# Issuing the v loads of 18 chunks from ScalarE's queue, in a gated-attention and gMLP kernel

## The chip, the cores and the metric

The kernel runs on one core of a Trainium2 chip. A core has five engines, each with a queue of its own that it works off strictly in order: TensorE (PE), VectorE (DVE), ScalarE (ACT), GpSimd (POOL) and SyncE (SP). SP computes nothing; it issues DMAs. The metric is the device time of one execution in microseconds (us), as the median of several runs.

## The reference

The inputs q, k, v and alpha have the shape (4, 8, 768, 48): batch, heads, steps, head size, in float32. For each batch and head a gated linear attention runs over the steps:

```
state = alpha[t][:, None] * state + outer(k[t], v[t])
y[t]  = q[t] @ state
```

The heads are then put side by side to x (4 x 768 x 384), and a gated MLP follows:

```
h = relu(x @ w_in);  u, v = h[..., :512], h[..., 512:]
v_n = (v - mean(v)) / sqrt(var(v) + 1e-6)
v_s = w_spatial @ v_n + b_spatial        # over the 768 steps
out = (u * v_s) @ w_out
```

## The kernel before, in words

**Tiles and stages.** The 768 steps of a batch are cut into chunks of 128, so there are 24 chunks, numbered 0 to 23 over the four batches. Chunks 0 to 5 are handled two at a time (`pair`, line 388), chunks 6 to 23 singly (`first`, line 590). A chunk has four loads: alpha (tile `ac`), k (`kc`), q (`qc`) and v (`vc`). A single chunk's load is 192 KB in pieces of 192 bytes (line 602); a pair's is 384 KB in pieces of 384 bytes (line 406). The tiles of a load rotate through three buffers, each of which holds two chunks, so a load waits until the reader of the chunks six places earlier is done.

For a single chunk the steps are these. ACT takes the logarithm of alpha (`ln`, line 616) and PE makes its running sum (`cum`, 622 and 625). ACT takes exponentials of it (`einv` 634, `ebc` 641, `eexp` 651). POOL multiplies k by one of them (`kt`, 646) and DVE multiplies q by the other (`qt`, 656). v is cast to bf16 (`vb`, 663, by ACT or POOL, through the helper at line 196 or 198). PE transposes kt and qt (`trk`, 672 and 674), and the result is copied to SBUF (`ev`). PE makes the scores (`sc`, 704), DVE masks them (`m`, 715), PE updates the state from kt and vb (`upd`, 690) and makes y (`y`, 726 and 732). DVE and POOL keep the state (`z`, `S`, `sb`; lines 325 to 340). y is copied, transposed and copied to `xT` (`xs`, `xt`, `xe`; lines 353 to 372).

The MLP of a batch runs in groups of matmuls at line 778: `v` and `u` (x by the two halves of w_in; the eviction with relu is on ACT or DVE), the normalisation of v (`bn`, `rs`, `vn`), `s` (the spatial product with w_spatial, evicted by DVE at 920, and a product with u on POOL or DVE at 933), and `o` (the product with w_out, evicted by ACT). Then the 128 x 384 result is stored (line 980). The weights come in six pieces of 768 KB (line 1008): two of w_in, three of w_spatial, one of w_out. They go through two buffers, are cast to bf16, and w_spatial is transposed on PE.

**What sets the order.** Every step is an operation with a number and the engines that may do it. The constant `PLAN` (line 57) is an order table written out in full: a word such as `P54:512` says that operation 54 comes next and is done by PE (P PE, D DVE, A ACT, G POOL, S an issue on SP, Q the landing of a DMA, which emits nothing), and that before it 512 columns of junk matmul are run on PE (line 188). `replay` (line 111) emits the operations in this order. Each engine's queue therefore has its operations in the order of the table, and an engine that waits for one operation holds up all that follow it in its queue. A DMA is two operations, its issue and its landing (`dma`, line 295); the issue is on SP unless said otherwise.

**Queues.** All loads and stores but one are issued by SP; POOL issues the load of b_spatial (line 1028).

Of the kernel before, what the change touches and what calls it, by code (L numbers as in the profile page):

```python
# [57 lines left out]
S34 S96 G0 S36 S38 Q35 D1 Q97 S100 A42 Q37 S98 P43:512:512:512:512:512:512:512:512:512:352 A104 G32 P54:512 Q33 A44  # L58
Q39 S40 P116 A55 D47 A56 P105:128 A57 G58 A45 A46 D2 Q101 S166 P50:512:96 A107 A106 P61:256 A117 D51 A118 A108 D59
A119 Q99 S102 D48 P63:512:512:512:512 A64 D121 P243:512:224 P52 D110 P125 Q41 S4 D53 D62 A126 P73:512:512:160 G120  # L60
P114 A244 D74 P76 Q167 G109 S168 P123:160 D115 D75 A49 G60 P112:512:512:192 D77 Q103 A113 P65:224 S170 D78 A124
P135:512 D66 A174 P79:96 D136 G67 Q5 S172 P138 A80 D137 G68 P69:224 A111 D70 G122 D139 P83:512:352 G71 D140 P175 G72
Q169 S9 P127 A177 A84 P81 D128 P141 A82 G129 A176 P85 Q171 S303 P186 A142 D7 G6 A86 P131 D8 A178 P143 D130 G179 A187
P87 Q173 S14 A188 D132 P90 A88 G133 D180 P145 A91 G189 D190 Q10 S305 A144 P182 D92 P184 A146 G134 P194 A185 P149
D195 G181 A183 D89 P147 P192 G191 A148 P200 G3 Q304 A193 S307 P245:128 D201 P160 A150 D202 Q15 P203 P196 D12 A13 D11
A246 D205 P156:512:512:512:512:320 S18 A93 P154 D197 A311 Q306 S309 D204 A161 G198 P152 A157 P312 D16 Q308 G199 S335
A155 P206 D151 A313 G17 Q19 A153 P210 D94 A314 A207 G315 D162 S22 P158 A316 P208 A211 P233 D317 A209 P231 D95 A163
P212 Q310 P319 D232 S337 A213 P214 D164 A234 G20 D320 Q336 P223 S370 A215 G21 D159 P217 Q23 D216 S339 P227 A218 P235
A224 P237 D219 A228 P225 A318 P229 D165 A343 Q338 D236 S341 P325 A220 D238 P321 A226 P344 Q371 D222 P259 A230 S372
D221 P251 A346 A345 D326 Q340 A24 G25 P255 S374 D322 P256 D327 A348 Q342 P260 G347 S412 D257 P239 A378 Q373 P328  # L70
G323 P241 S410 A240 D349 P379 P252 Q375 D261 A380 S414 P247 A381 D242 A329 G262 Q413 P248 A350 D253 S376 A383 P351
D249 G324 Q411 P353 P330 D352 S26 P267 A331 G258 P268 D384 Q415 S445 P357 G382 D269 P275 Q377 A418 D354 S416 P276
D359 G355 P386 Q27 D358 G356 S447 P271 D387 P419 G254 P272 A421 D277 A420 P392 A423 G422 P332 D424 P360 D273 G250
Q446 A333 S449 P426 D393 A361 P263 G274 A385 Q417 D394 P264 S477 A427 P388 P362 D265 Q448 P395 S479 A363 D31 P432
G266 D30 A396 P364 Q450 D29 A28 S481 D389 A453 D334 P397 P279 G390 Q478 A398 S572 G391 A365 P454 D433 P399 Q480 A455
D434 G278 S451 A456 A458 P408 A400 Q482 P283 D459 G425 S574 A280 D401 G457 P404 A284 Q573 P287 S604 A485 D409 G270
A405 Q452 P428 D366 P486 A288 S576 P435 A487 P461 Q575 A436 G488 S483 P291 A367 D462 A489 Q605 P295 D369 S578 A292
D429 P437 D490 A296 Q577 P467 G430 S606 A438 P406 D368 G431 A580 D469 P492 Q484 A407 S608 P581 D468 G460 P439 A582
Q579 D493 A583 S641 A585 P463 G584 P470 D464 A612 Q607 P494 D586 A471 S639 P402 G465 D495 A440 P472 Q609 G466 P613
A403 D496 S679 P588 A615 A614 G491 P299 D441 Q642 A473 S610 G587 A617 P497 G616 D589 Q640 P474 A498 S681 D618 A442  # L80
P590 P499 Q680 D591 P594 A500 S715 P620 G592 D596 A300 Q611 P501 A475 D443 S645 A476 D621 P514 Q682 P508 S643 D595
A502 P512 A503 Q716 G619 D444 S683 D515 P626 A647 P597 D504 P524 Q646 A513 S717 P528 A598 A509 Q644 D627 P540 S685
A505 P648 A687 P599 D507 Q684 P510 A600 D506 S719 P688 A649 D628 P525 Q718 A650 A690 A652 G651 S747 P541 D526 A723
P622 Q686 P529 D542 A689 G593 S749 A692 P544 D623 D530 Q720 A654 G691 P545 S751 D693 P629 D653 Q748 G624 P724 S841
P695 D511 A725 G543 P655 A630 Q750 D546 P516 S873 A726 A728 G527 P631 D696 A656 Q752 P517 S721 G625 P657 D729 P601
A632 Q842 D658 A694 G531 S843 D518 P661 A602 P701 Q874 D662 P633 G727 A755 S845 D663 P520 Q722 A634 G519 D702 S875
P756 P521 A757 Q844 D703 G659 P664 S877 P536 D522 G758 A665 Q846 P731 D635 A759 S753 P532 G660 A849 Q876 D760 P666
P697 S912 G547 P533 A667 D698 A732 Q878 P537 D534 S908 G523 P704 D538 P850 Q754 A705 P668 D603 G699 S948 A851 P762
A852 Q913 A854 G853 S847 P677 A669 D855 P706 Q909 A730 P548 G700 D678 S301 A707 D763 P733 Q949 P857 A549 D734 S879
A881 P708 D858 G735 A670 Q848 P737 S983 G535 P764 A709 D739 P863 Q302 P671 A710 S914 G736 D738 Q880 P552 S910 A636  # L90
D765 G761 P740 A672 Q984 G539 D766 P882 S950 A741 P556 A553 D864 Q915 G856 P767 S1015 A557 D865 P742 P560 A884 A768
Q911 D711 A883 S952 P673 A886 G885 P564 Q951 A743 D887 S985 A916 P769 D637 G888 P859 A561 Q1016 P675 D674 G923 S954
A770 P744 D676 A712 Q953 P777 D860 S987 A745 D638 P889 G861 Q986 A565 P771 S1019 A956 D890 A778 P779 Q955 D746 A772
S289 P917 P891 P957 A919 Q988 A918 D713 P866 S989 D714 A959 P781 A780 G920 D773 A921 Q1020 P793 S1021 A867 P797 D892
A1023 Q290 D922 P568 A774 S293 Q990 A958 P924 S1017 D776 A961 P785 D775 G960 Q1022 A782 D925 P868 S285 P786 A869
D962 G893 P794 Q294 A963 D787 G862 P798 A569 Q1018 D795 A991 P870 S570 G788 D799 S297 Q286 P926 A871 P895 D927 G796
P930 Q571 D897 P801 Q298 G894 P802 D896 P783 D932 G928 P992 D931 P789 A994 A993 P898 D803 A784 G995 P1024 A996 P966
P933 A899 D967 P790 D997 A934 G968 P809 A1025 D791 G998 A1027 P900 P810 D872 G1026 A901 P964 D1028 P999 G800 A965
P813 D1000 G792 P935 P1030 D811 A936 P814 D1031 G804 P1001 P817 D1002 G929 D815 P970 A818 P1005 D971 P1032 G1003
P942 G1029 D972 P821 G816 D1006 P805 A822 D1007 G969 P973 P937 D1033 A974 G1004 P806 D1034 A938 P975 P1008 D807 A976  # L100
P902 D943 A1009 G808 D939 P1035 A903 P1010 P977 G812 A1036 D904 P944 A978 P940 A1011 D979 P1037 P829 A1038 D945 A905
P825 D907 P1012 A826 A980 P1039 A941 D981 P1049 A1013 D982 P946 D906 A1040 D1014 P1045 A830 P1051 A947 S831 D1041
A1046 P1047 S281 P1053 S823 D1050 A1042 Q832 S558 P1057 A1052 D1044 Q282 S827 P1077 A1048 D1043 Q824 S562 P1065 Q559
P1078 S819 P1066 Q828 P1061 Q563 D1067 P1054 Q820 G1068 P1058 D1055 P1062 D1059 G1056 P1069 D1060 P1070 D1063 P1073
D1079 P833 P1074 A834 P1081 D1075 S835 P1082 D1064 S550 G1076 P837 S554 D1071 Q836 S566 P1084 D1080 A838 Q551 G1072
P1088 S839 Q555 D1083 A1085 P1092 Q567 S1086 A1089 Q840 P1100 S1090 A1093 Q1087 P1096 S1094 A1101 Q1091 P1104 S1102
A1097 Q1095 S1098 A1105 Q1103 S1106 Q1099 Q1107
# [16 lines left out]
def kernel(  # L124
# [12 lines left out]
    nc = tc.nc  # L137

    B, H, S, D = q.shape
    C = 128  # L140
# [50 lines left out]

    ENG = {"ACT": nc.scalar, "DVE": nc.vector, "POOL": nc.gpsimd}
# [195 lines left out]
    def pair(j):  # L388
# [13 lines left out]
        def load(name, src):  # L402
            def emit(_):
                t = st[name] = io_pool.tile([128, 2, H, D], FP32, name=name).rearrange(
                    "p a h d -> p (a h d)").rearrange("p (h a d) -> p h a d", h=H, a=2)
                nc.sync.dma_start(
                    out=t.rearrange("p h a d -> p h (a d)"),
                    in_=src[b, :, t0:t0 + 2 * C, :].rearrange("h (p a) d -> p h (a d)", a=2))
            return emit
# [180 lines left out]
    def first(i):  # L590
# [6 lines left out]
        def load(name, src):  # L597
            def emit(_):
                if i % 2 == 0:
                    T[i + 1][name + "2"] = st[name + "2"] = io_pool.tile([128, 2, H, D], FP32, name=name)  # L600
                t = st[name] = st[name + "2"][:, i % 2]
                nc.sync.dma_start(out=t, in_=src[b, :, t0:t0 + C, :].rearrange("h s d -> s h d"))  # L602
            return emit
# [6 lines left out]
        dma(("vc", i), LD, load("vc", v), io_users("vb", j), P + 0.3)  # L610
# [340 lines left out]
    def second_o(b, tt):  # L951
# [27 lines left out]
        def store(_):  # L979
            nc.sync.dma_start(out=out[b, tt * 128:(tt + 1) * 128, :], in_=hold["o"])  # L980
# [19 lines left out]
    def fetch(key, prio, to, src):  # L1000
# [4 lines left out]
        def load(_):  # L1005
            flat = raws.tile([128, n * cols], FP32, name="raw_w")
            hold["w"] = flat.rearrange("p (n f) -> p n f", n=n)
            nc.sync.dma_start(out=hold["w"], in_=src)
# [75 lines left out]
```

## Time and profile before

| | |
|---|---|
| median of 3 runs | 147.5 us (146.93 to 147.93) |
| the profiled execution | 148.49 us, its span 146.7 us |
| granted TensorE clock, mean | 0.997 of full |
| PE busy | 138.6 us (94%) |
| DVE, ACT, POOL busy | 120.6, 107.8, 87.1 us |
| matmuls of the groups (line 778) | 38% of the chain that ended last |
| junk matmuls (line 188) | 66, 11.8 us busy |
| issues of vc on SP, single chunks | 18, median 4.2 us from issue to landing |
| HBM read, written | 23.60 MB, 4.72 MB |

The profile page is made from one execution. Its span runs from the first to the last instruction of the program; the rest of the execution's time lies around it. The page gives the busy time of each engine, the same in 40 slices, the DMA queues, the chain of work that ended last (followed back from the last instruction, at each step to what released it), and the costliest groups of instructions. A group is named by line, engine, operation and out<-in; after the bar stand its busy time, the mean of one in ns, and the idle time of the engine just before them with what ended it. An issue of a DMA is shown on the queue of its issuer ("SPq") and is not counted as busy. PE's busy time is modelled, so a PE that is 99% busy is not at its peak; how much useful work is done is counted in columns of the matmuls instead.

### The profile page before, as it was taken

The numbers are of one execution on the slowest core, as the hardware profiler recorded it, in microseconds if no ns is written. First come the engines' busy times: TensorE is split into PE (matmuls) and PEld (weight loads), VectorE is DVE, ScalarE is ACT, GpSimd is POOL, SyncE is SP. The second block draws the span as 40 slices with busy tenths as digits, with TensorE's granted clock in tenths as the row PEclk, the third lists the DMA queues.
The fourth block names the chain that finished last, engine by engine and source line by source line (L and its number), as shares of the span: only waits on it lengthen the run. The fifth ranks groups of instructions, "written<-read, shape, count | busy, mean of one in ns | idle before, by whom it ended". The sixth has DMA issues, their size and how long they took to land.

```text
span 146.7 us, 4486 instructions
## 1 busy us (share of the span) xinstructions
PE 138.6 (94%) x1702; PEld 92.3 (63%) x1715; DVE 120.6 (82%) x260; ACT 107.8 (73%) x271; POOL 87.1 (59%) x148
## 2 busy tenths in 40 slices
PE   6999999999999999995998999999999999999990
PEld 3567776676666666773666577666667766566550
DVE  6578989979999899994977898988989999767820
ACT  3595779988984599995996889999948548860160
POOL 5726487574258959773139987853597994004320
PEclk9999999999999999999999999999999999999998
DMA  4999998978997999997998999999998000063384
GB/s 109 268 261 263 330 259 245 332 183 210 312 216 151 267 208 199 197 197 141 191 213 163 221 194 206 186 210 188 202 222 258 22 0 0 4 242 138 135 293 161
DMA packets 93014, 28.61 MB, mean 195 GB/s; under 512 B 87872, under 2 KB 91456, under 8 KB 92992
## 3 DMA queue, kind: packets, MB, share of 16 engines
q1 hardware_dynamic: 92960, 28.32, 83.4%
q8 instruction: 13, 0.21, 0.6%
q14 instruction: 9, 0.07, 0.2%
q0 software_dynamic: 32, 0.00, 0.0%
HBM read 23.60 MB, written 4.72 MB: 193 GB/s over the span
## 4 chain that ended last, share of the span: by engine, by line
PE 64%; DMA 12%; DVE 8%; ACT 5%; POOL 4%; issue 3%; SPq 1%; DVEq 0%; ACTq 0%; POOLq 0%
PE bank L778 38%; DMA qc<-in_q_dram 7%; PE bank L188 6%; DMA raw_w<-in_moe_w_spatial_dram 5%; PE bank L704 2%; POOL gT L933 2%; PE bank L672 2%; PE bank L732 2%; PE bank L361 2%; PE bank L674 2%; PE bank L690 1%; DVE qt L656 1%; PE bank L492 1%; PE bank L428 1%; SPq L602 1%
## 5 line engine op out<-in xcount | busy, mean ns | idle before, releaser
L778 PE MATMUL bank<-w_spT,vn 128*128 128x384 bf16 x192 | 36.3, 326 | 0.0
L933 POOL TENSOR_TENSOR gT<-vsb,uT 128x384 bf16<-128x384 f32 x28 | 25.8, 932 | 16.1 <-DVE vsb L920 15.5
L778 PEld LDWEIGHTS <-vn 128*128 128x128 bf16 x192 | 17.3, 97 | 10.0 <-issue 0.2
L715 DVE TENSOR_TENSOR ptm<-bank,mask 128x512 bf16<-128x512 f32 x36 | 22.8, 681 | 0.5 <-PE bank L704 0.5
L646 POOL TENSOR_TENSOR kt<-kc,binv 128x384 bf16<-128x384 f32 x18 | 16.7, 928 | 7.4 <-ACT bc L641 4.4
L920 DVE TENSOR_TENSOR vsb<-bank,bsp_bc 128x384 f32<-128x384 f32 x31 | 16.7, 552 | 3.8 <-PE bank L778 2.8
L778 PE MATMUL bank<-xT,w_in 128*128 128x384 bf16 x96 | 19.2, 327 | 0.0
L778 PE MATMUL bank<-w_out_sb,gT 128*128 128x384 bf16 x96 | 18.4, 326 | 0.1
L778 PE MATMUL bank<-w_in,xT 128*128 128x512 bf16 x59 | 17.1, 379 | 1.0 <-issue 0.5
L332 POOL TENSOR_TENSOR state<-state,bc 128x192 f32<-128x192 f32 x20 | 10.2, 511 | 8.2 <-DVE state L327 4.9
L198 POOL CAST sbd<-state 64x192 bf16<-64x192 f32 x38 | 12.9, 340 | 2.0
L196 ACT COPY xT<-bank 128x384 bf16<-128x384 bf16 x24 | 11.7, 487 | 3.0 <-PE bank L361 2.4
L839 DVE BATCH_NORM_STATS2 stats<-v_sb 128x6 f32<-128x512 bf16 x20 | 13.6, 682 | 0.3 <-ACT v_sb L202 0.3
L202 ACT ACTIVATE v_sb<-bank 128x512 bf16<-128x512 f32 x20 | 11.7, 598 | 2.6 <-PE bank L778 2.2
L656 DVE TENSOR_TENSOR qt<-qc,bank 128x384 bf16<-128x384 f32 x18 | 9.8, 548 | 4.4 <-DMA qc<-in_q_dram 2.9
L188 PE MATMUL bank<-junk 128*128 128x384 bf16 (+5 forms) x66 | 11.8, 313 | 1.3 <-DVE junk L231 1.3
L198 DVE COPY kqT<-bank 128x1024 bf16<-128x1024 bf16 (+1 forms) x19 | 11.6, 614 | 1.5 <-PE bank L674 0.5
L196 ACT COPY o_sb<-bank 128x384 f32<-128x384 f32 x9 | 4.3, 480 | 11.4 <-PE bank L778 11.4
L778 PEld LDWEIGHTS <-w_in 128*128 128x128 bf16 x96 | 8.7, 98 | 6.1
L778 PEld LDWEIGHTS <-gT 128*128 128x128 bf16 x96 | 9.0, 97 | 5.4 <-issue 0.3
L196 ACT CAST x_sb<-bank 128x384 bf16<-128x384 f32 x24 | 11.6, 488 | 1.0 <-PE bank L732 0.5
L871 DVE TENSOR_SCALAR vn<-v_sb,mvs,rstd 128x512 bf16<-128x512 bf16 x24 | 10.6, 467 | 2.0 <-ACT rstd L864 1.9
(124 smaller groups left out, 299.1 us busy)
## 6 DMA issues: line engine op xcount, KB each, us to landing
ac<-in_alpha_dram SPq DMA_DIRECT2D x18, 192.0 KB, 4.1
kc<-in_k_dram SPq DMA_DIRECT2D x18, 192.0 KB, 3.9
qc<-in_q_dram SPq DMA_DIRECT2D x18, 192.0 KB, 3.8
vc<-in_v_dram SPq DMA_DIRECT2D x18, 192.0 KB, 4.2
raw_w<-in_moe_w_spatial_dram SPq DMA_DIRECT2D x3, 768.0 KB, 7.6
out_dram<-raw_w SPq DMA_DIRECT2D x12, 192.0 KB, 2.3
out_dram<-o_sb SPq DMA_DIRECT2D x9, 192.0 KB, 2.4
raw_w<-in_moe_w_in_dram SPq DMA_DIRECT2D x2, 768.0 KB, 7.6
```

Of the source, the lines that this page charges most:

```text
L188: nc.tensor.matmul(out=flat[:, 0:n], lhsT=junk[:, 0:128], rhs=junk[:, 0:n], start=True, stop=True)
L196: nc.scalar.copy(out=out, in_=in_)
L198: ENG[eng].tensor_copy(out=out, in_=in_)
L202: nc.scalar.activation(out=out, in_=in_, func=AF.Relu)
L646: ENG[eng].tensor_mul(out=k_blocks(kt3)[:, :, :, 0:D], in0=quad(st["kc"]), in1=st["binv"])
L656: nc.vector.tensor_mul(out=qt[:, :, ::-1, 0:D], in0=quad(st["qc"]), in1=st["cv"])
L715: nc.vector.tensor_tensor(out=st["ptm"][:, s], in0=st[f"pt{s}"], in1=mask4, op=ALU.mult)
L778: return lambda ps: nc.tensor.matmul(out=out(ps), lhsT=lhsT(), rhs=rhs(), start=start, stop=stop)
L839: nc.vector.bn_stats(out=stats, in_=d["v_sb"][:, tt, :])
L871: nc.vector.tensor_scalar(out=d["vn"][:, t, :], in0=d["v_sb"][:, t, :], scalar1=d["mvs"][:, t, 0:1], scalar2=d["rstd"][:, t:t + 1], op0=AL ...
L920: nc.vector.tensor_tensor(out=hold["vs"], in0=ps[:, 0:TH], in1=bsp_bc[:, th, :], op=ALU.add)
L933: ENG[eng].tensor_tensor(out=bt[b]["gT"][:, dsl, cols], in0=hold["vs"], in1=bt[b]["uT"][:, dsl, cols], op=ALU.mult)
```

## The change

The loads of v of the single chunks (6 to 23) are issued by ACT's queue instead of SP's: `dma(("vc", i), ...)` gets `eng="ACT"`, and the function that issues takes the queue from the engine that the table names. The 18 issues become instructions of ACT, in ACT's order. The loads of the pairs (also v), of the weights, and the stores stay on SP.

The table is replaced by another one for two queues. It has the same 1108 operations. Beside the 18 issues it moves these:

- casts of v: ACT 7 to 4, POOL 11 to 14 (single chunks); ACT 2 to 3, POOL 4 to 3 (pairs)
- `ev` of single chunks: ACT 4 to 6, DVE 14 to 12; of the pairs' k: ACT 4 to 2, DVE 2 to 4; of their q: ACT 3 to 4, DVE 3 to 2
- k product of the pairs: POOL 5 to 2, DVE 1 to 4
- casts of weights: w_in ACT 1 to 3, DVE 4 to 2; w_spatial ACT 1 to 0, DVE 1 to 2; w_out DVE 3 to 2, POOL 0 to 1
- transposed w_spatial: ACT 2 to 3, DVE 4 to 3; one state copy and one product with u from POOL to DVE
- junk columns: 16224 to 18976

The order of issues changes as well. SP's queue begins like this before and after (the number is the chunk, the first of two for a pair; `w_sp` is w_spatial):

```
before: ac0 ac2 kc0 qc0 qc2 kc2 vc0 ac4 vc2 w_in.1 kc4 qc4 vc4 w_in.0 ac6 w_sp.0 kc6 qc6 w_sp.1 vc6 ac7 w_sp.2 kc7 ac8 qc7 vc7 kc8 qc8
after:  vc0 ac0 ac2 kc0 kc2 qc0 qc2 vc2 ac4 qc4 w_in.1 kc4 ac6 vc4 ac7 w_in.0 ac8 w_sp.0 qc6 kc6 ac9 qc7 kc7 w_sp.1 w_sp.2 kc8 qc8
```

In the new table the issues of vc6, vc7 and vc8 on ACT stand ahead of w_in.0, of kc6 and of kc6, in that order. Around them ACT's queue reads: `xs.0 vc.6.issue eexpp.2.1 ... xe.3 xe.2 vc.7.issue vc.8.issue vbp.2.1 ln.6`.

The diff, with the table cut to its first line:

```
 PLAN = """
-S34 S96 G0 S36 S38 Q35 D1 Q97 S100 A42 Q37 S98 P43:512:512:512:512:512:512:512:512:512:352 A104 G32 P54:512 Q33 A44
...
+S40 S34 G0 S96 S36 Q41 D1 Q35 S98 D2 Q97 S38 A42 G32 A49 G60 Q37 S100
...
+    QUEUE = {"SP": nc.sync, "ACT": nc.scalar}
     ENG = {"ACT": nc.scalar, "DVE": nc.vector, "POOL": nc.gpsimd}
...
         def load(name, src):
-            def emit(_):
+            def emit(eng):
                 if i % 2 == 0:
                     T[i + 1][name + "2"] = st[name + "2"] = io_pool.tile([128, 2, H, D], FP32, name=name)
                 t = st[name] = st[name + "2"][:, i % 2]
-                nc.sync.dma_start(out=t, in_=src[b, :, t0:t0 + C, :].rearrange("h s d -> s h d"))
+                QUEUE[eng].dma_start(out=t, in_=src[b, :, t0:t0 + C, :].rearrange("h s d -> s h d"))
...
-        dma(("vc", i), LD, load("vc", v), io_users("vb", j), P + 0.3)
+        dma(("vc", i), LD, load("vc", v), io_users("vb", j), P + 0.3, eng="ACT")
```

The loads of the pairs, the stores and the weights' loads get the same `QUEUE[eng]`, with SP as the engine.

## The prediction

> **What bounds the kernel now.** I read the page first: span, engine rows, DMA row.
>
> ```profile
> span 146.7 us, 4486 instructions
> ...
> PE 138.6 (94%) x1702; PEld 92.3 (63%) x1715; DVE 120.6 (82%) x260; ACT 107.8 (73%) x271; POOL 87.1 (59%) x148
> ...
> DMA  4999998978997999997998999999998000063384
> ...
> GB/s 109 268 261 263 330 259 245 332 183 210 312 216 151 267 208 199 197 197 141 191 213 163 221 194 206 186 210 188 202 222 258 22 0 0 4 242 138 135 293 161
> ...
> q1 hardware_dynamic: 92960, 28.32, 83.4%
> ```
>
> The DMA engines are full from the start to about 113 us and then nearly idle. Before that the rate sits near 200 GB/s wherever only chunk loads run. The profiled execution took 148.49 us, its span 146.7, the runs' median is 147.5: I work with differences against the span and add them to the median.
>
> Next, the busy time by stage (columns: PE, PEld, DVE, ACT, POOL, clock, DMA share, GB/s):
>
> ```profile
> 24.00:56.00 32.00, 31.35 (x407) 21.30 (x409) 29.92 (x64) 25.98 (x64) 20.65 (x34) 1.00 0.98 236
> 56.00:80.00 24.00, 21.95 (x275) 14.90 (x276) 19.47 (x45) 20.77 (x59) 14.63 (x26) 1.00 0.96 187
> 80.00:112.00 32.00, 31.78 (x402) 21.83 (x406) 28.63 (x62) 27.77 (x74) 23.40 (x38) 1.00 0.98 201
> 112.00:146.70 34.70, 30.91 (x267) 19.20 (x265) 23.70 (x50) 17.18 (x41) 14.29 (x22) 0.99 0.34 123
> ```
>
> TensorE (PE) loses 2.05 us between 56 and 80 us (24.00 - 21.95), 0.65 between 24 and 56, and almost nothing from 80 on. ACT is idle for 6.02 + 3.23 + 4.23 = 13.5 us between 24 and 112. Who makes PE wait is in the chain in order of time, and in the view of the v tiles:
>
> ```profile
> 63.81 5.16 DMA qc<-in_q_dram
> 68.97 0.03 issue
> 69.00 0.02 DVEq L656
> 69.02 0.04 issue
> 69.06 0.55 DVE qt L656
> ...
> 73.89 4.87 DMA qc<-in_q_dram
> ...
> 78.86 1.03 DVE qt L656 x2
> ...
> 125.97 17.06 PE bank L778 x101
> ```
>
> ```profile
> L602 SPq DMA_DIRECT2D vc<-in_v_dram x18: 425/888/2058, 30.2 to 106.6; - x18
> ...
>   PE bank L690: 1.1, 1
> ...
> DMA to landing us min/median/max: 3.8/4.3/7.5
> ```
>
> So the kernel is PE-bound, with PE work held up wherever a load is late. 101 matmuls in 17.06 us are 0.17 us each. With 384 columns in 0.163 us (three in 0.49 in the chain), the order tables of before and after hold the same useful PE work, 125.8 us by their columns: the new time is decided only by how much PE waits and by the start and the end.
>
> **The change part by part.**
>
> *The transfers themselves: 0 us.* The bytes and the 192-byte pieces stay. Two windows of 8 us give the price of a load: one single chunk's load, 196,608 B, takes 0.99 us at 199 GB/s (56 to 64 us), a pair's takes 1.48 us at 266 GB/s (8 to 16 us). The engines' share there is 1.01 and more, so a second queue finds no free engine: a v load that goes sooner makes a k or q load later by 0.99 us. What it can fill is the rest, a DMA share of 0.96 to 0.98 in the three stages: 0.02 x 32 + 0.04 x 24 + 0.02 x 32 = 2.2 us at most. [...]
>
> *The order of loads on SP: +1.8 us.* The new table is another order, not the old one minus 18 issues. By the table's places, chunk 6 (the first single chunk) suffers. Ahead of its k load now stand six more single loads: alpha of 7 and 8, q of 6, and v of 6, 7 and 8 on ACT's queue. That is 6 x 0.99 = 5.9 us.
>
> ```profile
> 23.06 0.59 SPq L602 DMA_DIRECT2D kc<-in_k_dram  x1
> ...
> DMA to landing us min/median/max: 3.9/4.8/7.8
> ...
> ```
>
> ```profile
> 31.62 0.90 POOL L646 TENSOR_TENSOR kt<-kc,binv 128x384 bf16<-128x384 f32 x1
> ```
>
> ```profile
> 33.60 0.39 PE L672 MATMUL bank<-ident,kt 128*128 128x128 bf16 x4
> ```
>
> Before, this k load was issued at 23.06 and took 7.8 us (the longest of four in the k tiles' view), so it landed at 30.9; its product on POOL started at 31.6 and its transposes on PE at 33.6. After, the landing is 30.9 + 5.9 = 36.8, or 3 x 0.99 less (33.8) if ACT reaches its v issues later than the table thinks. With 0.90 of POOL and 0.2 of hand-over the transposes start at 37.9, or at 34.9. The PE work ahead of them in the table is 21.1 us against 20.5 before, so by there PE has waited 37.9 - 33.6 - 0.6 = 3.7 us more, or 34.9 - 33.6 - 0.6 = 0.7: 2.2 in the middle. The weights move too: w_spatial's second part has 8 more single loads ahead of it (7.9 us), w_out about as many; the matmuls that need them stand 2 to 4.5 us later in PE's table and 2.2 us later in time, which covers all but a few tenths. From chunk 7 on the sets loaded are about the same. The old stall (2.05 us at 56 to 80) was for v of chunk 12 and q of 13 and 15. In the new table q of 15 comes some 6.5 us later by its place, but PE has 5.2 us more work ahead of chunk 15's transposes (68.0 against 62.8) and is 2.2 us later: nearly even. I book a gain of 0.4 there: 2.2 - 0.4 = +1.8. Ends: -2.7 (all of 2.05 + 0.65 goes, chunk 6 covered) and +3.7.
>
> *The start: 0 us.* SP's first load is now v of the first pair, so the first alpha lands one pair load (1.48 us) later and q of the first pair two later (3.0). The late chunk 6 covers it, as do 2752 more junk columns. Without that cover the start costs up to 1.5 us, and what replaces it as late is w_in's first half, also behind three more single loads.
>
> *ACT: +1.7 us.* ACT gets 18 issues. No row shows an issue on ACT. Lower end: the shortest of the 72 issues on SP at this line, 0.376 us (least of the queue ahead of it): 6.8 us. Upper end: 1.44 us, the median for v of a pair in the same view, which has to wait for transfers ahead: 26 us. ACT's own queue holds few transfers, but the 16 engines are those that SP keeps full, so I take the median of the same instruction, 0.89: 16.0 us. Beside this, moved evictions add 1.7 us to ACT by its mean durations (3 v casts fewer at 0.41, 2 kqT copies more at 0.94, 2 weight casts more at 0.50, and small ones). Up to the ln of chunk 12 ACT has no trouble: 46.2 us of work and 6 issues, against 46.8 us that before were done at 62.1 us. From there to the xT copy of chunk 18 (before: 44.3 us, of them 39.2 busy) it has 42.8 us and 11 issues: 52.6 us at 0.89, 8.3 over; at 0.376 it is 46.9, 2.6 over. What queues behind each issue is ln, exp and the evictions; for these wait kt on POOL, qt on DVE and then PE. Not all of it is on the path: 2 us are given by the later loads, o and u evictions (12 x 0.4 us in that stretch) have no near reader, and PE has S and O groups to run meanwhile. Between 0 (2.6 - 2) and 6.3 (8.3 - 2) I take 1.7, nearer to the low end, as 4.8 us are such evictions. [...]
>
> *POOL and DVE: 0 us.* POOL gets 3 more v casts (0.50 each) and 3 kt of pairs fewer (0.91); DVE gets these 3. POOL is busy 59%; on DVE it falls in the start, where PE runs junk; if not covered, +0.6 each.
>
> *SP: 0 us.* It issues 18 fewer, but its issues are as long as the DMA lets them be (mean 0.99 us, as the transfer), so they only spread.
>
> Sum: 147.5 + 0 + 1.8 + 0 + 1.7 = **151.0 us**.
>
> **The rivals.**
>
> *The v wait goes and nothing replaces it (faster).* A v load no longer stands behind SP's full queue (median 4.3 us to landing); the 1.1 us that PE waited for a v cast and the q waits vanish because q moves up. 147.5 - 2.7 = 144.8. Against it: the DMA share of 0.96 to 1.01. It decides if chunk 6's transposes start by 34.5 and PE loses under 0.7 us between 56 and 80.
>
> *ACT becomes the bound (slower still).* With issues of 1.2 us, 42.8 + 13.2 = 56.0 against 44.3: 11.7 over, less 2 from the loads and 4.8 of evictions that may wait, 4.9 us, on top of 1.8: 154.2; at 1.44 it is 156.8. For it: SP's issues last up to 3 us when transfers stand ahead of them. Against it: ACT's queue is its own. It decides from about 0.9 us an issue.
>
> *Nothing moves (about 147.5).* Chunk 6's delay is eaten by two queues filling the 2.2 us of gaps, and issues are short. The split of issues itself is certain from the program's order, so "the change does not take place" is excluded.
>
> **How the numbers follow.** About 1% (1.5 us, three runs of before spread over 1.0) is what a measurement can tell. Forecast (149.0 to 153.5): 0.47. ACT as bound (over 153.5): 0.18. Faster (under 146.0): 0.18. Nothing moves (146.0 to 149.0): 0.17. So faster 0.18, same 0.17, slower 0.65. The range 145.0 to 157.0 takes in all but the ends of the outer two (0.07 below, 0.06 above); the likeliest case alone is 149.0 to 153.5.
>
> **What would show it.** Right: single loads still about 0.99 us apart at 195 to 205 GB/s; transposes of chunk 6 at 35 to 38 us; useful PE work equal, PE's loss moved from 56-80 us to 24-40 us; ACT issues of 0.4 to 1.2 us and ACT idle under 5 us from 62 to 112. Wrong: a DMA rate over 210 GB/s in the chunk stage (two queues do move more), ACT issues near 0.1 us, or a last k or q load that lands clearly before 111 us.

## The result and the profile after

The kernel after takes 152.94 us (median of 4 runs, 151.44 to 153.35), the kernel before in the same session 147.72 us (146.93 to 148.13). The ratio is 1.034, with a 95% interval of 1.026 to 1.043: the change makes the kernel about 5 us slower. Ratios and their intervals come from all executions but those over 1.5% above the fastest of their kernel, so they can differ a little from the quotient of the medians. The profiled execution of after took 153.35 us, its span 151.6 us against 146.7.

The page of after, with the rows that the prediction showed of before:

```profile
span 151.6 us, 4500 instructions
...
PE 140.8 (93%) x1712; PEld 92.5 (61%) x1725; DVE 122.6 (81%) x262; ACT 109.3 (72%) x272; POOL 83.7 (55%) x145
...
DMA  4999999998989999799999999970590200049134
GB/s 118 265 261 263 275 271 280 349 243 150 335 210 202 218 292 219 148 216 219 192 262 199 229 229 226 229 133 0 160 205 9 52 0 2 4 147 366 60 144 167
...
q1 hardware_dynamic: 74240, 24.78, 68.7%
q10 hardware_dynamic: 18720, 3.54, 12.0%
```

Read the last two rows first: there are two queues now, and q10 carries the 18 loads of v (3.54 MB). The DMA row drops at about 101 us, and the rate to 0: SP then stands at a store whose data isn't there yet, with a single load (q of chunk 23) behind it. The last load of k lands at 100.8 us, before at 113.0. By 101 us all but 6 of the 72 single loads have landed, before all but 11; q of chunk 23 and v of chunks 20 to 23 are issued only from 106 us on, and the last of them lands at 118.9 us. Most loads are done sooner, and yet the span is 4.9 us longer. So the loads' throughput isn't what became worse.

The busy time by stage (PE, PEld, DVE, ACT, POOL, clock, DMA share, GB/s):

```profile
0.00:24.00 24.00, 22.09 (x348) 14.77 (x348) 17.83 (x42) 15.47 (x35) 12.83 (x33) 1.00 1.10 244
24.00:56.00 32.00, 29.73 (x405) 20.37 (x407) 27.71 (x61) 25.51 (x62) 17.80 (x28) 1.00 1.04 250
56.00:80.00 24.00, 21.54 (x265) 13.74 (x263) 19.24 (x41) 19.90 (x53) 15.61 (x29) 1.00 1.05 214
80.00:112.00 32.00, 31.84 (x375) 21.39 (x378) 27.37 (x61) 28.77 (x81) 21.05 (x34) 1.00 0.85 179
112.00:151.60 39.60, 35.58 (x334) 22.18 (x335) 30.46 (x62) 19.62 (x46) 16.36 (x25) 1.00 0.30 98
```

PE loses 2.27 us between 24 and 56 (before: 0.65) and 2.46 between 56 and 80 (before: 2.05). The rate is higher than before in both stages: 250 against 236 and 214 against 187 GB/s.

Who makes PE wait in the first of them is in the chain in order of time (start, length, what):

```profile
26.89 9.38 DMA kc<-in_k_dram
...
36.41 0.92 POOL kt L648
...
37.38 0.40 PE bank L674 x4
```

This is chunk 6: its k load lands at 36.28 us, its product on POOL follows, and its transposes start at 37.4 us, against 33.6 before. But PE itself stood still for it for less than that. PE's timeline gives the idle time in front of these transposes in brackets:

```profile
37.38 0.40 PE L674 MATMUL bank<-ident,kt 128*128 128x128 bf16 x4 [0.93 <-POOL kt L648]
```

Up to 0.93 us before, PE was working off what stands ahead of them in its order. So the late load holds PE up by 0.93 us at most; the rest of the 3.8 us PE brings with it.

In the second stage, the chain has a row that before couldn't have: an issue on ACT that waits for a load. The waits of ACT give the size (us in total, times, longest):

```profile
63.03 5.08 DMA kc<-in_k_dram
68.11 0.02 issue
68.13 0.37 ACTq L604
```

```profile
ACT raw_w L198 <- DMA kc<-in_k_dram: 2.4, 1, 2.4
```

ACT stands still for 2.4 us in front of an eviction (`raw_w`). PE soon waits for what ACT does next, the copy to `x_sb`:

```profile
69.51 0.34 PE L363 MATMUL bank<-ident,x_sb 128*128 128x128 bf16 x3 [1.72 <-ACT x_sb L198]
```

The eviction needs no k load. What waited was the issue ahead of it in ACT's queue, the v load of chunk 13; it starts 0.02 us after a load of k has landed. That v issue needs no k load either. The trace's records of the issues, with the semaphores that they raise and wait for, show why it waits. In before, the 114 DMAs that SP issues raise eight completion semaphores (counters that tell of a landing) in strict turn, and each issue from the ninth on waits, by itself or in a semaphore instruction ahead of it, for its own semaphore: for the DMA eight issues earlier. That DMA was issued 9.1 us earlier in the median and had landed at least 2.8 us before, so no issue stood still for it. In after, the 96 DMAs of SP and the 18 of ACT raise eight semaphores between them, 14 or 15 DMAs each, and each issue again waits for its own. The v issue of chunk 13 raises number 103, and the DMA before it on 103 is SP's load of k of chunk 13, issued only 5.1 us earlier, at 63.03, and landed at 68.11 us. It works the other way too: SP's issue of k of chunk 7, also on 103, starts 0.02 us after the landing of v of chunk 7, which ACT had issued; there SP loses only 0.1 us.

The issues themselves took 0.375 us in the median (ns, min/median/max, first and last start):

```profile
L604 ACTq DMA_DIRECT2D vc<-in_v_dram x18: 374/375/540, 21.4 to 116.1; - x18
```

### The profile page after: what moved, and what is told of

It reads as the page before. It is cut to its first block, busy times and chain, and to the rows that moved or that the text cites. A ratio compares the mean times of both kernels' runs of the same rounds, so it can differ in the third digit from the quotient of the medians.

```text
span 151.6 us, 4500 instructions
## 1 busy us (share of the span) xinstructions
PE 140.8 (93%) x1712; PEld 92.5 (61%) x1725; DVE 122.6 (81%) x262; ACT 109.3 (72%) x272; POOL 83.7 (55%) x145
## 3 DMA queue, kind: packets, MB, share of 16 engines
q10 hardware_dynamic: 18720, 3.54, 12.0%
## 4 chain that ended last, share of the span: by engine, by line
PE 68%; DMA 13%; ACT 7%; SPq 4%; DVE 3%; issue 2%; POOL 1%; ACTq 0%; DVEq 0%; POOLq 0%
PE bank L780 41%; DMA kc<-in_k_dram 10%; SPq L604 3%; PE bank L189 3%; DMA ac<-in_alpha_dram 3%; PE bank L706 2%; PE bank L674 2%; PE bank L363 2%; PE bank L734 2%; PE bank L676 2%; PE bank L692 2%; PE bank L624 2%; PE bank L494 2%; PE bank L430 2%; PE bank L728 1%
## 5 line engine op out<-in xcount | busy, mean ns | idle before, releaser
L935 POOL TENSOR_TENSOR gT<-vsb,uT 128x384 bf16<-128x384 f32 x27 | 24.6, 920 | 16.9 <-DVE vsb L922 11.1
L780 PE MATMUL bank<-xT,w_in 128*128 128x384 bf16 x96 | 19.8, 325 | 0.0
L780 PE MATMUL bank<-w_in,xT 128*128 128x512 bf16 x59 | 17.6, 379 | 1.0 <-issue 0.3
L334 POOL TENSOR_TENSOR state<-state,bc 128x192 f32<-128x192 f32 x20 | 10.5, 525 | 10.8 <-DVE state L327 5.2
L189 PE MATMUL bank<-junk 128*128 128x384 bf16 (+3 forms) x76 | 12.8, 310 | 1.6 <-DVE junk L233 1.3
L200 POOL CAST sbd<-state 64x192 bf16<-64x192 f32 x36 | 12.8, 355 | 1.9
L200 DVE COPY kqT<-bank 128x1024 bf16<-128x1024 bf16 (+1 forms) x18 | 10.6, 593 | 2.8 <-PE bank L676 2.1
L636 ACT ACTIVATE binv<-bank 128x384 bf16<-128x384 f32 x18 | 8.8, 496 | 4.8 <-POOL vb L200 3.1
L204 ACT ACTIVATE uT<-bank 128x384 bf16<-128x384 f32 x22 | 11.0, 498 | 0.9 <-PE bank L780 0.9
```

Source lines behind the costliest of these rows:

```text
L189: nc.tensor.matmul(out=flat[:, 0:n], lhsT=junk[:, 0:128], rhs=junk[:, 0:n], start=True, stop=True)
L200: ENG[eng].tensor_copy(out=out, in_=in_)
L204: nc.scalar.activation(out=out, in_=in_, func=AF.Relu)
L334: ENG[eng].tensor_tensor(out=st["state"], in0=st["state"], in1=st["bc"][:, :, None].to_broadcast([128, HP, D]), op=ALU.mult)
L780: return lambda ps: nc.tensor.matmul(out=out(ps), lhsT=lhsT(), rhs=rhs(), start=start, stop=stop)
L935: ENG[eng].tensor_tensor(out=bt[b]["gT"][:, dsl, cols], in0=hold["vs"], in1=bt[b]["uT"][:, dsl, cols], op=ALU.mult)
```

## The experiments

The runs fall into four sessions, and in each the kernel before was timed too. Its median was 148.35 us in the first (the first four runs below), 148.18 in the second (the v issues moved in the table, and the loads alone), 148.65 in the third (the pins, and chunk 6 with its weight) and 148.79 in the last (the repaired order). Ratios are to the kernel before of the same session. Theory at the start: the new order of loads costs the time, by the late chunk 6, and the second queue next to nothing. Rivals: the second queue itself (waits in ACT's queue, DMA time taken from k and q), or the start.

### The old table with v on ACT

```
-... S309 ...
+... A309 ...        # vc.6.issue; likewise the 17 others
...
+        dma(("vc", i), ..., eng="ACT")
```

The letter of the 18 v issues is changed at the same places of the old table, and `QUEUE` is added as in the change.

> The table of before, word for word in its order, with the 18 v issues given to ACT instead of SP. Theory (the new order of loads costs the time, the second queue next to nothing, since each of the 18 issues took 0.375 us and ran beside the ACT instruction ahead of it): 146 to 148.5 us, transposes of chunk 6 at 33 to 35 us. Rival (the second queue itself costs the time, by waits in ACT's queue and by v loads that push k and q loads back): 150 to 154 us, with ACT idle for several microseconds just before issues.

Measured: 151.66 us (150.29 to 152.21), ratio 1.023 (1.016 to 1.030). My theory missed by 3 us: the second queue alone costs. Up to chunk 13 the kernel is ahead of before (transposes at 67.8 us against 69.7; in a second measurement of the same program, told below, 68.9), so loads of v on a queue of their own seem to help there. Then ACT waits four times, by 0.8 to 1.5 us, 4.5 us in all. The chain of this run shows the longest:

```profile
70.01 4.73 DMA kc<-in_k_dram
74.74 0.02 issue
74.76 0.37 ACTq L603
```

Again the v issue (of chunk 15) starts 0.02 us after the landing of a k load, which SP had issued 4.75 us before (74.76 - 70.01). After the wait ahead of this one (1.0 us, at v of chunk 14) and after this one, PE stands still for ACT:

```profile
73.71 0.32 PE L623 MATMUL bank<-la,ut_ones 128*128 128x384 bf16 x1 [1.04 <-ACT uT L203]
...
76.18 0.32 PE L623 MATMUL bank<-la,ut_ones 128*128 128x384 bf16 x1 [1.39 <-ACT la L617]
```

By chunk 18 the lead is gone (93.0 against 91.2 us).

### The new table with v on SP

The reverse: the table of after, with the letter of the 18 issues back to S.

> The new table, with the 18 v issues back on SP at the same places of the table. Theory (order of loads): 152 to 155 us, no better than the changed kernel, since the order is kept and the gain of a second queue is lost. Rival (second queue): 147 to 149.5 us.

Measured: 151.67 us (151.43 to 151.99), ratio 1.024 (1.019 to 1.030). That is just under the range that I had given (152 to 155, no better than after), so neither side has it all: the new order without the second queue costs 3.3 us (151.67 - 148.35), and the queue the rest. The rest is small: the intervals of this run and of after overlap. The run with alpha first (next section), which differs from after in two issues of SP only, was timed in the same session and lies clearly above: 153.05 us (152.71 to 153.8), 1.4 us more. The stages of this run:

```profile
0.00:24.00 24.00, 21.82 (x345) 14.63 (x346) 17.71 (x42) 15.31 (x34) 12.88 (x33) 1.00 1.07 242
24.00:56.00 32.00, 29.45 (x396) 19.98 (x398) 27.28 (x59) 25.28 (x62) 17.72 (x28) 1.00 0.98 235
56.00:80.00 24.00, 23.14 (x292) 15.18 (x293) 21.52 (x47) 21.49 (x58) 16.37 (x29) 1.00 0.95 199
```

The loss between 24 and 56 us is there as in after (2.55 against 2.27 us). The one between 56 and 80 isn't (0.86 against 2.46). In the new order, the early loss belongs to the order itself, the later one to the queue.

### Alpha first, and k and q of chunk 6 first

```
alpha_first:   ac0 vc0 ac2 kc0 ...            (after: vc0 ac0 ac2 kc0 ...)
chunk6_first:  ... ac7 w_in.0 kc6 qc6 ac8 w_sp.0 ...
```

> The changed kernel with the first two issues on SP swapped: alpha of the first pair, then v, as the first is needed for everything. First running sum on PE 1.5 us sooner (at 5.6 instead of 7.0 us). Theory (the start is covered by the late load of chunk 6): 152.3 to 153.3 us, no change by over 0.5 us. Rival (the start is on the path): about 1.5 us less, 151.4 us.

> The changed kernel with the issues of k and q of chunk 6 moved to just behind that of the second half of w_in, ahead of alpha of 8, w_spatial's first part and, in time, v of 7 and 8. Theory (chunk 6's late k load costs 3.2 us of PE's waiting): k of chunk 6 lands at 30 to 33 us instead of 36.3, its transposes start at 33 to 35 instead of 37.4, time 149.5 to 151.5 us. Rival (the start of the kernel is late anyway and chunk 6's load only stands in front of it): transposes come sooner but the time falls by less than 0.7 us.

Measured: alpha first 153.05 us (152.71 to 153.8), ratio 1.034, no difference to after. Chunk 6 first 154.19 us (153.39 to 154.99), ratio 1.041: a miss. Its k load landed at 30.3 us, 6 us sooner, and the transposes started at 38.3. POOL's own order held the product: it first casts w_spatial's first part, which now landed later (35.4 us against 32.7), and PE stood still for this cast itself for 1.96 us.

### Moving the v issues four SP issues earlier in the table

```
old table, before the edit:  ... ac6 w_sp.0 kc6 qc6 w_sp.1 [vc6] ac7 ...
after it:                    ... ac6 [vc6] w_sp.0 kc6 qc6 w_sp.1 ac7 ...
```

So for each v issue (in brackets, on ACT), in both tables; the order within each engine stays.

> The kernel after, with every engine's order of instructions as it is; only the place of each v issue in the table moves four issues of SP earlier, so that the completion semaphore that it takes in the round of eight was last used by an older load. Theory (ACT's 2.4 us idle ahead of the v issue of chunk 13 is the wait for the load eight places earlier in the table, and it is all that the second queue costs here): that idle time goes, no v issue is preceded by over 0.5 us of ACT idle that a load ends, and the time is 150.5 to 152.0 us, level with the new order on one queue (151.7). Rival (the cost of the queue is v loads that take DMA time from k and q): the idle time goes, the last k and q loads stay as late, and the time stays at 152.5 to 153.5 us.

> The old table with the 18 v issues on ACT, as in the run of that kind before, with every engine's order kept and only the place of each v issue in the table moved four issues of SP earlier (an older load is the one whose semaphore it waits for). Theory (the 3.2 to 4 us that the second queue cost in the old order are ACT's waits for older loads): the four idle stretches of ACT of 0.8 to 1.5 us ahead of v issues go, chunk 18's transposes start by 91 us, and the time is 146.0 to 148.5 us. Rival (ACT's issues themselves, or v loads that take DMA time from k and q): ACT's waits go and the time stays at 150 to 152 us.

Measured: in the new table 151.55 us (149.78 to 152.91), with the 2.4 us of ACT gone; the spread is too wide for a verdict. A wait of the other kind came up there: SP's issue of w_spatial's first part stood still until v of chunk 6, which ACT had issued, had landed, 1.8 us:

```profile
SPq L1009 <- DMA vc<-in_v_dram: 1.8, 1, 1.8
```

In the old table 150.75 us (150.38 to 151.58), ratio 1.020 (1.015 to 1.025), with the waits where they had been. The reason is that the edit did nothing there: the program came out the same as that of the old table with v on ACT. It is a second measurement of that kernel. The edit in the new table moved the tiles to other buffers too, so neither run separates the theories.

### Pinning the v issues: fewer waits of ACT

Where a v issue falls in the round of the eight semaphores can be set: an edge that orders without waiting is added between a v issue and the SP issues around it. Each is put where ACT came to it in the trace of the earlier run. All five engines' orders stay as they were, and so do the buffers; in the programs only semaphores and waits differ, SP's among them.

```
+BEHIND = "..."      # pairs x:y, x comes behind y in the program's sequence
...
+    for pair in BEHIND.split():
+        x, y = map(int, pair.split(":"))
+        tc.add_manual_dep(ins[x], ins[y].name, NOSYNC, reason="order")
```

> The old table with the 18 v issues on ACT; every engine's order of instructions is that of the earlier run of that kind. Changed is only where each v issue falls in the round of the eight completion semaphores: it is pinned to the place in the sequence of SP's issues at which ACT came to it in that run, so that the load eight places earlier has landed by then. Theory (what the second queue costs in the old order is ACT waiting for the landing of a load of SP): the four idle stretches of 0.8 to 1.5 us ahead of v issues go, chunk 18's transposes start by 91 us, and the time is 146.0 to 148.5 us. Rival (v loads that take DMA time from k and q, or ACT's issues themselves): the waits go and the time stays at 150 to 152 us.

> The kernel after with every engine's order and every buffer as it is; each v issue is pinned to the place in the sequence of SP's issues at which ACT came to it, so that its completion semaphore's last load has landed. Theory: ACT's 2.4 us ahead of the v issue of chunk 13 go, and the time is 150.5 to 152.0 us, that of the new order with one queue (151.7) or up to 1 us less. Rival (the queue's cost is DMA time taken from k and q): 152.5 to 153.5 us.

Measured: the old table 149.11 us (148.18 to 150.77), ratio 1.004 (1.001 to 1.007), where the same engine orders had 1.023 and 1.020. The new table 151.41 us (150.86 to 152.32), ratio 1.022 (1.017 to 1.027), where after had 1.034 (and alpha first, the same but for two issues, 1.029 to 1.040); with v on SP it was 1.024. So in both orders most of the cost of the second queue goes with these waits, with not one instruction moved on any engine. PE's idle time for ACT goes with them: the 1.04 and 1.39 us of the old order and the 1.72 us of the new one are gone. The theory of the waits holds, and both rivals fall: the v loads still run beside those of k and q (in the new order they are the 3.54 MB of q10), and ACT still issues them. Waits of SP don't explain it: in the old order no issue of SP started right at the landing of a v load, with pins or without.

The old table came out 0.6 us above the upper end that I had set, though chunk 18's transposes started at 90.8 us, as expected. The pins didn't free ACT altogether. In the old order two waits in front of v issues were left, 2.5 us in all where there had been four with 4.5 us; the longer one, at chunk 20, is new:

```profile
ACT rstd L882 <- DMA kc<-in_k_dram: 1.5, 1, 1.5
...
ACT la L635 <- DMA qc<-in_q_dram: 1.0, 1, 1.0
```

PE is at 23.93 of 24 us between 56 and 80 us there, the best of all runs, and gives some of it back later:

```profile
56.00:80.00 24.00, 23.93 (x299) 16.26 (x298) 21.92 (x49) 22.20 (x64) 15.87 (x28) 1.00 1.07 208
80.00:112.00 32.00, 30.29 (x362) 20.05 (x360) 26.51 (x58) 25.84 (x69) 22.26 (x37) 1.00 0.95 198
```

In the new order with pins, one shorter wait is left, at the v issue of chunk 15, behind which PE stands still for 1.1 us. What the second queue would cost or give without any such wait is not shown.

### Chunk 6 and its weight first, and the repaired order

```
after:                     ... ac6 vc4 ac7 [vc6] w_in.0 ac8 w_sp.0 qc6 [vc7 vc8] kc6 ac9 ...
chunk6_and_weight_first:   ... ac6 vc4 ac7 [vc6] w_in.0 kc6 qc6 w_sp.0 ac8 ac9 [vc7 vc8] ...
new_order_repaired:        ... ac6 vc4 w_in.0 ac7 kc6 qc6 [vc6] w_sp.0 ac8 ac9 [vc7 vc8] ...
```

In brackets are the issues on ACT, at their place in the table. The last one also has the pins.

> The kernel after with SP's k and q loads of chunk 6 and w_spatial's first part put ahead of alpha of chunk 8, and ACT's v issues of chunks 7 and 8 some ten ACT instructions later: loads that nobody reads before 34 us move behind those that PE's table needs at 33 to 35 us. The engines' other orders stay. Theory (the new order costs its 3 us because k of chunk 6 and the weight part that PE transposes just before come late): chunk 6's transposes start at 34 to 35.5 us in place of 37.4, and the time is 149.5 to 151.0 us. Rival (the delay at chunk 6 is only the first place where a general lateness shows, and is lost again by chunk 12 or 13): chunk 6 starts as early, chunk 13's transposes stay at 74 to 75.5 us, and the time is 152 to 153.5 us.

Measured: 153.95 us (152.24 to 154.16), ratio 1.036 (1.028 to 1.043): a miss. The loads came in time (k of chunk 6 at 30.0 us, q at 30.7) and the transposes started at 37.1. The chain of this run shows what holds them now:

```profile
35.26 0.51 DVE uT L205
35.77 0.47 DVE qt L657
36.24 0.04 issue
36.28 0.38 PE bank L188 x2
...
37.30 0.22 PE bank L673 x4
```

It is DVE's product for q, which stands in DVE's order behind the normalisation and a u eviction of the MLP's first groups; PE stood still for it for 0.7 us. Then come 0.9 us of PE's own work ahead of the transposes, 0.5 us of it junk columns (L188). Behind the late load stood a second thing that was as late. What was gained by chunk 9 (52.9 us against 53.6) went by chunk 15: ACT waited 2.4 us at the v issue of chunk 13 as in after, and 1.3 us more at that of chunk 15.

> The run with k and q of chunk 6 and w_spatial's first part put forward, with three edits more: w_in's second part (the first half by columns of the matmul) is issued ahead of alpha of chunk 7, the v issue of chunk 6 stands five ACT instructions later, and each later v issue is pinned to the place in the sequence of SP's issues at which ACT came to it, so that ACT doesn't wait for older loads. PE's, DVE's and POOL's orders stay those of the kernel after. Theory (the new order loses in its first 56 us, where loads that nobody needs yet stand ahead of the weights and of chunk 6, and ACT's waits took back what the run before had gained there): PE's useful work by 56 us is at least 42.5 us (after: 39.8, before: 43.4), and the time is 149.0 to 150.5 us. Rival (PE's, DVE's and POOL's own order in the new table is what costs, wherever the loads land): 151.0 us or more.

Measured: 154.91 us (153.09 to 155.44), ratio 1.041 (1.034 to 1.049): the opposite of what I had expected. Both waits of ACT were gone, but now w_spatial's first part landed at 36.27 us instead of 33.27, since SP's issue of q of chunk 6 ahead of it lasted 3.63 us. POOL and through it PE (2.8 us) stood waiting for it:

```profile
36.32 1.60 POOL L217 CAST w_row<-raw_w 128x768 bf16<-128x768 f32 x2 [5.22 <-DMA raw_w<-in_moe_w_spatial_dram]
```

The run supports neither side: the weight came late in it. What its rival says (that the other engines' orders cost, wherever the loads land) isn't refuted.

### Loads alone, with one queue and with two

```
+        eng = nc.scalar if TWO and n % 4 == 3 else nc.sync
+        eng.dma_start(out=t, in_=src[...])
```

> Leaves out the whole computation: it only loads 60 single chunks (alpha, k, q and v in turn, 196,608 bytes each) in a row from SP and stores zeros. It shows what one queue moves without any compute beside it. Theory (the DMA engines are full with one queue): about 0.99 us a load, 199 GB/s, as in the kernel before from 56 to 64 us. Rival (the kernel's own waits held the rate down): 0.85 to 0.9 us a load, 220 GB/s or more.

> The same 60 loads and zeros, the computation left out as there, with every fourth one (v) issued by ACT. Theory of the prediction (a second queue finds no free engine): the same 0.99 us a load, 195 to 205 GB/s. Rival, for which the profile after speaks (up to 70 to 75 pieces a us on each DMA engine against 65): 0.87 to 0.92 us a load while both queues are active, 213 to 226 GB/s.

Each was executed once. The rates of the two, in 40 slices; the high ones at the end are the stores:

```profile
GB/s 2 204 212 200 202 212 214 203 199 217 208 193 208 191 221 203 206 211 206 192 230 210 207 216 211 213 183 208 202 209 196 9 261 365 370 363 371 362 371 20
```

```profile
GB/s 0 197 243 218 218 218 218 218 217 218 218 218 218 218 218 218 218 209 221 191 224 200 203 215 223 193 204 213 217 174 202 246 397 386 380 372 375 366 319 3
```

With one queue the 60 loads land at 3.69 to 59.80 us, 0.95 us each. With two, 28 land between 5.88 and 29.81 us, 0.89 us each, as long as both are active; the rest, on one queue, take 0.94. With one queue, my 0.99 us was nearer than the rival's 0.85 to 0.9. With two, the rival was right: two queues moved 7% more (0.95 / 0.89). But the loads got slower: the median from issue to landing rises from 3.8 to 4.8 us over all 60, and for v from 3.8 to 6.7 us. Divided by the spacing of the landings, the latter is an estimate of 4.0 loads under way with one queue (3.8 / 0.95) and, if all took as long as v, 7.5 with two (6.7 / 0.89). ACT's issues got longer too:

```profile
L23 ACTq DMA_DIRECT2D ld<-in_v_dram x15: 470/1748/1930, 0.7 to 23.1; - x15
```

## Why the prediction was right and where it was wrong

The direction and roughly the size were right: 151.0 us with a range of 145 to 157, and it is 152.94. Of the 5.2 us (152.94 - 147.72), the sum had 3.5. The split into order and queue holds, but neither of the two terms came about as I had described it, so that the sum came so near is in part luck. Step by step:

**The transfers themselves, 0 us.** The time is right, the reason isn't. I took the DMA share of 0.96 to 1.01 to mean that a second queue finds no free engine. Two queues moved more: 0.89 against 0.95 us a load in the loads-only runs, and in after 214 GB/s between 56 and 80 us (before 187), where I had named 210 as the bound that would prove me wrong. No run had shown that none of the 2.2 us of gaps would be won; what the runs then showed is that the higher rate buys no time: with most of ACT's waits gone, two queues and one are within 0.5 us of each other (149.11 against 148.65 us in the old order, 151.41 against 151.67 in the new). And in after, PE loses 2.46 us in that stage at 214 GB/s, before 2.05 at 187: a higher mean rate did not make PE wait less. The loads-only runs give what is saved in all, 7%; they don't tell the issuer's time from the engines', since SP's issues stand back to back with one queue.

**The order of loads, +1.8 us.** Measured +3.3 us by the new table with v on SP. The step's own figures came at their upper end: k of chunk 6 landed at 36.28 us (36.8 expected) and its transposes started at 37.4 (34.9 to 37.9). I took the middle, because I thought that ACT would reach its v issues late; it reached them in the table's places. But the step counted nearly all of the delay at chunk 6 as PE waiting for this load (3.7 us at its upper end), and PE waits 0.93 us for it. So the lateness isn't undone by mending this load. With its k load at 30 us, the transposes stay at 37 to 38: POOL's cast of the weight, then DVE's q product are as late. My step treated the load as the only thing that had moved. Which of the moved parts the 3.3 us belong to stays open: four runs with other load orders (alpha first, chunk 6 first, chunk 6 and its weight first, the repaired order) took nothing off, and other parts of the table (the engines' orders, the junk columns) were not changed one by one.

**The start, 0 us.** Alpha ahead of v changes nothing, as I had said for the first load. "Covered by the late chunk 6" is wrong. The first 24 us of before, and PE's busy time in them on the junk line alone (first number behind the length), before and after:

```profile
0.00:24.00 24.00, 22.63 (x365) 15.12 (x367) 18.86 (x44) 16.05 (x36) 14.12 (x32) 1.00 1.07 244
```

```profile
0.00:24.00 24.00, 10.44 (x56) 5.27 (x56) 1.00 1.07 244
```

```profile
0.00:24.00 24.00, 11.31 (x68) 6.24 (x68) 1.00 1.10 244
```

So PE's useful work up to 24 us is 12.2 us before (22.63 - 10.44) and 10.8 after (22.09 - 11.31); in the new table with v on SP it is 10.7 (21.82 - 11.16). A lag of 1.4 us, nearly half of the order's 3.3, is there before k of chunk 6 is needed. Counted in the same way up to 40 us, it is 2.7 us (26.5 against 23.9 us of useful work). What causes it (the order of the start's loads, the engines' orders, or the junk itself, 12.8 us in all against 11.8) no run tells apart.

**ACT, +1.7 us.** The size is about right (151.67 to 152.94 is +1.3, 1.4 within the one session; the pins take off 1.5), but by luck, as the mechanism is wrong. I charged 18 issues at 0.89 us. They take 0.375, the lower end, and mostly nothing at all, since they run beside the instruction ahead of them on ACT. What costs is one wait, 2.4 us in front of one issue, of which 1.72 us reach PE. The term's lower bound was a slip too: 2.6 - 2 is 0.6, not 0. I named "a queue of its own" as a point for ACT, and didn't look at what the two queues share: the completion semaphores. The 0.89 us, the median of the same instruction on SP, isn't seen on ACT in after: the 18 issues took 0.374 to 0.540 us, also beside an issue of SP (SP's of 25.27 to 26.28 us overlaps ACT's of 26.03 to 26.41). Longer ones are in the loads-only run with two queues: ACT's first issues there take 0.47, 0.74, 1.20 and 1.63 us, and 1.7 to 1.9 from then on. They start 1.6 us apart (15 between 0.7 and 23.1 us), in after 5.1 us apart in the median.

**POOL, DVE and SP, 0 us.** POOL waited less for v: in front of its casts 0.8 us once, before 5.3 us in four waits, and 1.8 us once in front of a product for the state (at 108.7 us). SP waited 0.1 us for a v load in after. DVE's place in the order did matter at chunk 6, as told above.

The rival that ends faster failed at its condition: chunk 6 was not in time. But in the old order its first half came true: a lead at chunk 13 was there (1.9 us, in the second measurement 0.8), until ACT's waits took it back. The rival of ACT as the bound wasn't needed, as the issues were short.

Of the signs that I had named, two more failed: PE's loss did not move from 56-80 us to 24-40 us but stands in both (2.46 and 1.42 us), and ACT was idle for 6.2 us between 62 and 112 us (50.00 - 43.75) and not under 5.

## What to carry to other kernels

Before moving issues to a second engine, look at what the two issuers share. Here the DMAs of SP and ACT raised the same eight completion semaphores: an issue of ACT waited until a k load of SP had landed, and the eviction behind it, which needs no k load, stood still with it for 2.4 us. A wait in front of an instruction that needs none is the mark of it: look at the queue's previous instruction. And a new order table moves many things at once, so mending the first late load shows the second. Read how long the engine itself stood still in front of the late instruction, and not how much later it started than before; and run the table without the other half of the change before explaining either.

## What the runs showed of the hardware

- In after, an issue on ACT ran beside the instruction ahead of it in ACT's queue. In the timeline (start, length, what) the issue at 26.03 lies within the copy that starts at 26.02, and the next copy starts at once:

```profile
26.02 0.48 ACT L198 COPY xT<-bank 128x384 bf16<-128x384 bf16 x1
26.03 0.38 ACTq L604 DMA_DIRECT2D vc<-in_v_dram  x1
26.40 0.48 ACT L198 COPY xT<-bank 128x384 bf16<-128x384 bf16 x1
```

- The issue of a v load of 192 KB on ACT took 0.375 us in the median in after, and 1.75 us where ACT issues v after v (loads alone, two queues). By the median time to landing and the spacing of the issues, an estimate of 0.8 such loads was under way at a time in after (4.1 / 5.1) and 4.2 there (6.7 / 1.6). In the loads-only run with one queue, SP's issues that follow each other start 0.94 us apart in the mean, about the 0.95 us of a load.
- In the repaired order, PE stood still for most of one slice while it waited for the weight, and the granted clock fell with it. The page's rows of PE and of the clock (tenths, 40 slices of 3.8 us):

```profile
PE   6999999992999999999999999999999999999990
...
PEclk9999999998579999999999999999999999999999
```

PE is busy two tenths of the tenth slice (34.5 to 38.3 us); the clock stands at 8, 5 and 7 tenths there and in the two slices behind it, where PE had work again. This seems to have added to the loss of that run: of its six executions, the one with a mean clock of 1.0 took 153.09 us, the five with 0.976 to 0.986 took 154.4 to 155.44. No other run here shows a lower clock in the middle of the span.
